# Folding the last chunk's score block and shifting three schedules in a gated attention and MoE kernel

## The chip, the cores and the metric

The kernel runs on one core of a Trainium2 chip. The metric is the device time of one execution in microseconds (us), as the median of several executions. Times of the profile ("span") are some 1.8 us shorter, because they run from the first instruction to the last one. A ratio of two kernels is the mean time of one kernel's runs over that of the other's of the same rounds, so it is not quite the ratio of the medians that are quoted.

## The reference

```python
# u, v: (8, 3008, 256), z: (8, 3008, 64), w_in: (256, 2048), w_out: (2048, 256)
scores = (1.0 / S) * np.matmul(z, z.transpose(0, 2, 1))
attn = np.maximum(scores, 0.0) ** 2
x = (u * np.matmul(attn, v)).reshape(B * S, D)
h = x @ w_in
g = h * (1.0 / (1.0 + np.exp(-1.702 * h)))
return g @ w_out
```

## The kernel before

The scores of a batch are symmetric. Each batch has 3008 rows of z in six chunks of 512 (the last has 448), and a "unit" is two blocks of 128 rows against one chunk: two matmuls of 64 contracted rows (two row tiles that run as a pair), a relu on ScalarE out of PSUM, and a square on VectorE. Blocks below the diagonal are not computed but made by DMA transposes (`tt`), and so is a quarter of each chunk's own block (`ad`, "folded"), except in batch 0 and in the last chunk. The matmuls of the second step, `o`, read a unit as right operand. TensorE runs a fixed list: units are scored ahead, at given "slots" (numbers of `o` steps within a chunk).

```python
    def scores(b, group):
        scs = []
        zt = ZT[b]
        for i, jp in group:
            sc = ps2.tile([P, 2, CH], F32, name="sc", tag="ps2")
            turn = turned(b, i) and jp >= NU - 2
            kp, qi = (2 * i + jp - (NU - 2), NCH - 1) if turn else (jp, i)
            q0, q1 = qi * CH, qi * CH + width(qi)
            if folded(b, i) and jp == 2 * i + 1:
                q0 += CH // 2
            for r in range(2):
                h = slice(r * DQK, (r + 1) * DQK)
                pe.matmul(
                    sc[:, r, :q1 - q0], zt[h, 2 * kp + r, :], zt[h].rearrange("d n p -> d (n p)")[:, q0:q1],
                    start=True, stop=True,
                )
            scs.append(sc)
    # ...
    def square(b, i, jp, sc):
        rl = pw.tile([P, 2, CH], F16, name="rl", tag="rl", bufs=3)
        if folded(b, i) and jp == 2 * i + 1:
            rh = rl[:, :, :CH // 2]
            act.activation(rh, sc[:, :, :CH // 2], AF.Relu, scale=csc)
            dve.tensor_tensor(unit[b, i, jp][:, 1], rh, rh, ALU.mult)
            return
        turn = turned(b, i) and jp >= NU - 2
        n = width(NCH - 1 if turn else i)
    # ...
        a = pa.tile([P, 2, CH], F16, name="a", tag="a", bufs=26)
        unit[b, i, jp] = a
        dve.tensor_tensor(a[:, :, :n], rl[:, :, :n], rl[:, :, :n], ALU.mult)
        if turn:
            twice = rl[:, :, LFULL:LAST]
            dve.tensor_tensor(a[:, :, LAST:], twice, twice, ALU.mult)
    # ...
        half = [(0, TOP, NJ - 1), (1, LOW, NJ - 1)]
        if both:
            order = [[(c, FULL, j)] for j in js[:-CB] for c in cs] + [[(c, FULL, j)] for c in cs for j in js[-CB:]]
            order.insert(-CB, half)
        elif i == full(b):
            order = [[(c, FULL, j)] for c in cs for j in js]
            order.insert(0 if i == NCH - 1 else len(order), half)
    # ...
    def pieces(b, i):

        lst = [(i, jp) for jp in range(2 * i, NU)]
        if i == NCH - 1:
            return [(i, jp) for jp in range(2 * i) if not turned(b, jp // 2)] + lst
        if b == 0:
            return lst[-2:] + lst[:-2] if turned(b, i) else lst
        k = max(len(lst) - 6, 2)
        return lst[:k] + lst[-2:] + lst[k:-2]
    # ...
    SCHED = {
        0: {n: 1 for n in (4, 9, 13, 17, 30, 33, 36, 39, 42, 45)} | {NJ: 2},
        1: {n: 1 for n in (5, 9, 13, 17)} | {NJ: 2},
        2: {n: 1 for n in (2, 7, 12, 17)} | {NJ: 2},
        3: {n: 1 for n in (6, 14, 32, 38)} | {NJ: 2},
        4: {},
        5: NEXT,
    }
    SCHED_LAST = SCHED | {3: {n: 1 for n in (14, 34)} | {NJ: 2}, 4: {NJ: 2}, 5: {}}
    # ...
        2: {n: 1 for n in (0, 3, 7, 11, 28, 32, 36, 40, 44)} | {NJ: 2},
    # ...
    keep_warm(7)
    for g in range(2):
        first_cast(g)
    for copies in [first_zt(g) for g in range(2)]:
        copies()
    posts = scores(0, [queue.pop(0) for _ in range(2)])
    turns = []
    for g in (2, 3):
        first_cast(g)
        keep_warm(2 * g - 2)
        turns.append(first_zt(g))
    for post_ in posts:
        post_()
    turns[0]()
    take(0, 1)
    load_u(0, 1)
```

`SCHED` has an entry for each chunk, in which `n: 1` means: ahead of step n, score one unit, and `NJ: 2` two units ahead of step 24. `SCHED0` (the single line) is for batch 0. Each batch scores two units (10 and 11) of the last chunk's own block. In batches 0 to 6 that is in chunk 3. `SCHED_LAST` is for batch 7, which has no batch after it to score ahead: there both are scored at `4: {NJ: 2}`, step 24 of chunk 4, and chunk 5 begins with `half`, which reads unit 11.

Of the kernel before, what the change touches and what calls it, by code (L numbers as in the profile page):

```python
# [10 lines left out]
F16 = mybir.dt.float16  # L11
P = 128
# [3 lines left out]
def kernel(  # L16
# [13 lines left out]
    AF = mybir.ActivationFunctionType  # L30
    ALU = mybir.AluOpType
# [5 lines left out]
    NJ = (S + P - 1) // P  # L37
    S0 = (S // P) * P
    SREM = S - S0
    CH = 512  # L40
# [12 lines left out]
    csc = 16.0  # L53
# [20 lines left out]
    nil = pw.tile([P, CH], F16, name="nil", tag="gf")  # L74
    dve.memset(nil, 0.0)

    late, LATE = [], []
    ZT, V16, UQ, UT, XT, unit, TT = {}, {}, {}, {}, {}, {}, {}

# [13 lines left out]
    def keep_warm(n):  # L93

        if "w" not in ZT:
            ZT["w"] = ps1.tile([P, CH], F32, name="w", tag="ps1")
        for k in range(n):
            pe.matmul(ZT["w"], nil[:, :P], nil, start=(k == 0), stop=(k == n - 1))  # L98
# [21 lines left out]
    def first_cast(g, by_act=False):  # L120
        m = g % CB * CB
        for c in range(2):
            dst, src = ZT["st"][g // CB][:, m:m + CB, c, :], ZT["f"][g // CB][:, m:m + CB, :]
            if by_act:
                act.activation(dst, src, AF.Copy, scale=1.0)
            else:
                dve.tensor_copy(dst, src)  # L127

    def first_zt(g):

        z2 = ZT["st"][g // CB][:, g % CB * CB:(g % CB + 1) * CB]
        zp = ps1.tile([P, CB, P], F16, name="zp", tag="ps1")
        for k in range(CB):
            pe.transpose(zp[:, k, :], z2[:, k, :, :], ident)  # L134

        def copies():
            zt = ZT[0][:, g * CB:(g + 1) * CB, :].rearrange("d n p -> d (n p)")
            nb = CB if g < NCH - 1 else CB - 1
            dst = zt[:, :nb * P].rearrange("d (p n) -> d p n", n=nb)
            src = zp[:, :nb, :].rearrange("d n p -> d p n")  # L140
            if g in (0, 2, 3):
                act.activation(dst, src, AF.Copy, scale=1.0)  # L142
            else:
                dve.tensor_copy(dst, src)  # L144
            if nb < CB:
                dve.tensor_copy(zt[:, nb * P:], zp[:, nb, :])

        return copies
# [65 lines left out]
    def folded(b, i):  # L214

        return i < NCH - 1 and b > 0

    def turned(b, i):

        return i < NCH - 1 and (b > 0 or i > 3)  # L220
# [6 lines that stand above are left out]
            turn = turned(b, i) and jp >= NU - 2  # L227
            kp, qi = (2 * i + jp - (NU - 2), NCH - 1) if turn else (jp, i)
            q0, q1 = qi * CH, qi * CH + width(qi)
            if folded(b, i) and jp == 2 * i + 1:  # L230
                q0 += CH // 2
            for r in range(2):
                h = slice(r * DQK, (r + 1) * DQK)
# [5 lines that stand above are left out]
        return [lambda u_=u_, sc=sc: square(b, *u_, sc) for u_, sc in zip(group, scs)]  # L239
# [5 lines that stand above are left out]
            act.activation(rh, sc[:, :, :CH // 2], AF.Relu, scale=csc)  # L245
            dve.tensor_tensor(unit[b, i, jp][:, 1], rh, rh, ALU.mult)
            return
        turn = turned(b, i) and jp >= NU - 2
        n = width(NCH - 1 if turn else i)
        act.activation(rl[:, :, :n], sc[:, :, :n], AF.Relu, scale=csc)  # L250
        if folded(b, i) and jp == 2 * i:
            a = pa.tile([P, CB, 2, P], F16, name="a", tag="a", bufs=26)
            unit[b, i, jp] = a
            r4 = rl.rearrange("p r (q c) -> p r q c", q=CB)
            dve.tensor_tensor(a.rearrange("p q r c -> p r q c"), r4, r4, ALU.mult)
            unit[b, i, jp + 1] = pa.tile([P, 2, 2, CH // 2], F16, name="ad", tag="a", bufs=26)
            sp.dma_start_transpose(
                unit[b, i, jp + 1][:, 0].rearrange("p g (r c) -> p (g r) c", c=P),
                a[:, CB // 2:].rearrange("p q r c -> p (q r c)"),
# [5 lines that stand above are left out]
        if turn:  # L265
            twice = rl[:, :, LFULL:LAST]
            dve.tensor_tensor(a[:, :, LAST:], twice, twice, ALU.mult)
        if jp // 2 > i and (turned(b, i) or jp < NU - 2):
            if b and i == 0 and LATE:
                late.append(((jp + 2) % NU, lambda: turn_unit(b, i, jp, a)))  # L270
            elif b == 0 and jp < NU - 2:
                squared.setdefault((i, jp // 2), []).append(lambda: turn_unit(b, i, jp, a))
                while ORDER0 and len(squared.get(ORDER0[0], ())) == 2:
                    for turn_it in squared.pop(ORDER0.pop(0)):
                        turn_it()
            else:
                turn_unit(b, i, jp, a)
# [257 lines left out]
    def store_part(b, k, o, c):  # L535

        r0 = b * S + k * CH
        y = Y[b, k].rearrange("p (m o) c -> p m o c", o=2)[:, :, o, c]
        if o == 0:
            dst = out[r0:r0 + 3 * P].rearrange("(s t) c -> t s c", t=P)[:, ::2, c]  # L540
            sp.dma_start(dst, y)
            return
        sp.dma_start(out[r0 + P:r0 + 2 * P, c], y[:, 0])
        for h in range(2):
            r1 = (b - h) * S + S0
            (act, pool)[h].dma_start(out[r1:r1 + SREM, c], y[h * SREM:(h + 1) * SREM, 1])

    def store(b, k, eng):
        i, n = blocks(b)[k]
# [13 lines left out]
    def pieces(b, i):  # L563
# [8 lines left out]

    NEXT = {n: 1 for n in (2, 6, 11, 15, 33, 37, 41, 45)} | {NJ: 2}
    SCHED = {
        0: {n: 1 for n in (4, 9, 13, 17, 30, 33, 36, 39, 42, 45)} | {NJ: 2},
        1: {n: 1 for n in (5, 9, 13, 17)} | {NJ: 2},
        2: {n: 1 for n in (2, 7, 12, 17)} | {NJ: 2},
        3: {n: 1 for n in (6, 14, 32, 38)} | {NJ: 2},
# [13 lines left out]
    SCHED0 = {  # L592
        0: {2: 1, 6: 2, 14: 2, 22: 2, 30: 2, 38: 2},
        1: {0: 2, 8: 2, 15: 2, 22: 2, 30: 2, 38: 2},
        2: {n: 1 for n in (0, 3, 7, 11, 28, 32, 36, 40, 44)} | {NJ: 2},
        3: {n: 1 for n in (0, 4, 8, 12, 16, 19, 29, 33, 37, 41, 45)} | {NJ: 2},
        4: {},
        5: NEXT,
# [4 lines left out]
    def take(b, n):  # L603
        for post_ in scores(b, [queue.pop(0) for _ in range(n)]):
            post_()
# [17 lines left out]
    for copies in [first_zt(g) for g in range(2)]:  # L623
        copies()
    posts = scores(0, [queue.pop(0) for _ in range(2)])
    turns = []
    for g in (2, 3):
        first_cast(g)
        keep_warm(2 * g - 2)
        turns.append(first_zt(g))  # L630
    for post_ in posts:
        post_()
    turns[0]()
    take(0, 1)
    load_u(0, 1)

    for b in range(B):
# [5 lines left out]
        for i in range(NCH):  # L643
            host = b + 1 if more and i == NCH - 1 else b
            if host > b:
                fill(host)
                LATE.append(host)
            for n, step in enumerate(attend(b, i, b == 0 and i < 2)):
                if b == 0 and i == 0 and n == 5:
                    load_u(0, 0)  # L650
                if b == 0 and i == 0 and n == 3:
                    turns[1]()
                if b == 0 and i == 0 and n in FIRST_CAST:
                    first_cast(FIRST_CAST[n], True)
                if b == 0 and i == 0 and n in FIRST_ZT:
                    first_zt(FIRST_ZT[n])()
                if (i, n) in turn:
                    turn_u(b, turn[i, n])
                if (i, n) in load:
                    load_u(b, load[i, n])  # L660
                if b == 0 and (i, n) in LOADW:
                    load_w(LOADW[i, n])
                if more and (i, n) == (NCH - 2, 2):
                    load_z(b + 1)
                if (b, i, n) == (0, NCH - 1, NJ + 4):
                    for sum_ in weight_sums():
                        sum_()
                take(host, sched[i].get(n, 0))
                if i == full(b) and n >= HEAD and (n - HEAD) * LAGY // (2 * NJ - 10) >= head and head < LAGY:
                    up_group(b, head)  # L670
                    head += 1
                step()
# [58 lines left out]
```

## Time and profile before

| | before |
|---|---|
| median of 3 runs | 1187.44 us (1186.94 to 1187.84) |
| span of the profile | 1186.0 us, mean granted clock 1.000 |
| TensorE busy | 1179.9 us (99%) |
| VectorE, ScalarE busy | 840.9 us (71%), 823.3 us (69%) |

TensorE is never without work for long, so the profile is read as a list of matmul starts: every part of the change must show as a shift of the same matmul between two traces. The lines are in the prediction. In all lines `sc` are the score matmuls, `hg` those with `w_in`, `st` and `yp` those with `w_out`, `rl` is a relu's output, and L234 is line 234 of the kernel.

### The profile page before, as it was taken

How to read it: one execution, taken by the hardware profiler on the slowest of the kernel's cores; microseconds unless marked ns; L12 is line 12 of the kernel's file. 1: busy time of each engine (PE TensorE's matmuls, PEld its weight loads, DVE VectorE, ACT ScalarE, POOL GpSimd, SP SyncE). 2: the span in 40 equal slices, each digit the busy share in tenths (PEclk: the TensorE clock that was granted, in tenths of full speed). 3: DMA queues.
4: the chain of work that ended last, by engine and by line, in shares of the span. 5: the costliest groups of instructions: out<-in, count | busy, mean ns of one | idle time of the engine just before them, and what ended most of it. 6: DMA issues, size and time to landing. Idle time of an engine off the chain costs nothing.

```text
span 1186.0 us, 27884 instructions
## 1 busy us (share of the span) xinstructions
PE 1179.9 (99%) x11529; PEld 723.9 (61%) x11529; DVE 840.9 (71%) x1433; ACT 823.3 (69%) x997; POOL 226.9 (19%) x321
## 2 busy tenths in 40 slices
PE   9999999999999999999999999999999999999998
PEld 3446765467654676547765478554775547855577
DVE  6788865877658776587765878648776587764776
ACT  7878864688646887478764787657876578672785
POOL 5243101231012310133101331014200141001000
PEclk9999999999999999999999999999999999999999
DMA  9997667666778687856789456895659856794012
GB/s 225 188 113 131 129 143 135 79 107 135 143 133 80 108 151 142 132 74 96 159 144 130 75 94 156 153 118 90 111 122 174 100 98 107 137 169 92 1 37 72
DMA packets 374175, 141.82 MB, mean 120 GB/s; under 512 B 315424, under 2 KB 367904, under 8 KB 374048
## 3 DMA queue, kind: packets, MB, share of 16 engines
q1 hardware_dynamic: 315856, 98.34, 45.3%
q0 software_dynamic: 56832, 40.45, 23.1%
q8 instruction: 90, 1.47, 0.5%
q10 hardware_dynamic: 1360, 1.25, 0.3%
q14 instruction: 37, 0.30, 0.1%
HBM read 60.29 MB, written 24.64 MB: 72 GB/s over the span
## 4 chain that ended last, share of the span: by engine, by line
PE 98%; ACT 1%; DVE 1%; issue 0%; DVEq 0%; ACTq 0%
PE o L348 40%; PE hg L389 27%; PE st L508 24%; PE sc L234 6%; PE yp L483 1%; ACT rl L250 1%; PE w L98 0%; PE zp L134 0%; DVE a L264 0%; DVE ut L201 0%; ACT gf L397 0%; DVE zst L127 0%; DVE WT L436 0%; DVE WT L437 0%; DVE ZT L144 0%
## 5 line engine op out<-in xcount | busy, mean ns | idle before, releaser
L397 ACT ACTIVATE gf<-hg 128x1024 f32<-128x1024 f32 (+1 forms) x384 | 385.9, 1005 | 138.6 <-PE hg L389 115.3
L250 ACT ACTIVATE rl<-sc 128x1024 f16<-128x1024 f32 (+1 forms) x309 | 294.9, 991 | 157.2 <-PE sc L234 110.9
L348 PEld LDWEIGHTS <-V 64*128 64x128 f16 (+1 forms) x4052 | 239.0, 94 | 233.7 <-issue 11.8
L389 PE MATMUL hg<-xt,W 128*128 128x512 f16 (+1 forms) x1408 | 354.6, 374 | 0.0
L401 DVE TENSOR_SCALAR gt<-gf 128x1024 f16<-128x1024 f32 (+1 forms) x320 | 223.8, 699 | 133.7 <-ACT gf L397 130.7
L348 PE MATMUL o<-a,V 64*128 64x512 f16 (+3 forms) x2286 | 302.8, 368 | 0.0
L264 DVE TENSOR_TENSOR a<-rl 128x1024 f16<-128x1024 f16 (+1 forms) x274 | 182.9, 671 | 128.7 <-ACT rl L250 128.1
L194 POOL DMA_DIRECT2D uq<-in_u_dram x188 | 127.7, 687 | 692.0 <-PE sc L234 455.7
L348 PE MATMUL o<-tt,V 64*128 64x512 f16 (+1 forms) x1510 | 234.0, 377 | 0.0
L389 PEld LDWEIGHTS <-W 128*128 128x128 f16 x1536 | 139.3, 98 | 119.3 <-issue 2.8
L508 PEld LDWEIGHTS <-gt 128*128 128x128 f16 x2944 | 177.1, 98 | 32.2
L508 PEld LDWEIGHTS <-s 128*128 128x128 f16 x2208 | 133.7, 98 | 25.6 <-issue 0.5
L234 PE MATMUL sc<-ZT 64*128 64x512 f16 (+2 forms) x688 | 118.5, 358 | 0.7 <-ACT ZT L142 0.3
L508 PE MATMUL st<-WT,gt 128*128 128x128 f16 x1472 | 97.8, 219 | 0.0
L508 PE MATMUL st<-WT,s 128*128 128x128 f16 x1472 | 96.5, 219 | 0.2 <-ACT uP L520 0.2
L508 PE MATMUL st<-W,gt 128*128 128x128 f16 x1472 | 96.5, 219 | 0.0
L526 DVE SCALAR_TENSOR_TENSOR y<-st,uP 128x256 f32<-128x256 f32 (+1 forms) x144 | 57.8, 408 | 28.3 <-ACT uP L520 19.9
L520 ACT ACTIVATE uP<-st 128x256 f32<-128x256 f32 (+1 forms) x144 | 53.1, 368 | 31.5 <-DVE y L526 16.2
L365 DVE TENSOR_TENSOR xt<-o,ut 128x512 f16<-128x512 f32 x80 | 51.4, 684 | 23.1 <-PE o L348 23.0
L399 ACT ACTIVATE gt<-gf 128x1024 f16<-128x1024 f32 (+1 forms) x64 | 65.9, 1030 | 2.1
L464 DVE TENSOR_TENSOR s<-s,gt 128x1024 f16<-128x1024 f16 (+1 forms) x96 | 65.0, 677 | 1.1
L462 DVE TENSOR_TENSOR s<-gt 128x1024 f16<-128x1024 f16 (+1 forms) x96 | 64.8, 675 | 0.0
(51 smaller groups left out, 590.9 us busy)
## 6 DMA issues: line engine op xcount, KB each, us to landing
out_dram<-y SPq DMA_DIRECT2D x40, 512.0 KB, 3.6
uq<-in_u_dram POOLq DMA_DIRECT2D x156, 128.0 KB, 3.6
V<-in_v_dram POOLq DMA_DIRECT2D x35, 256.0 KB, 6.4
tt<-a SPq DMA_TRANSPOSE x232, 3.7
uq<-in_u_dram POOLq DMA_DIRECT2D x32, 112.0 KB, 4.8
out_dram<-y SPq DMA_DIRECT2D x7, 384.0 KB, 3.1
vst<-in_v_dram SPq DMA_DIRECT2D x3, 512.0 KB, 5.5
zst<-in_z_dram POOLq DMA_DIRECT2D x7, 192.0 KB, 9.8
```

Source lines behind the costliest of these rows:

```text
L194: eng.dma_start(uq[k * QW:(k + 1) * QW, :n // QW].rearrange("t q c k -> t q (c k)"), src[:, :, cs])
L234: pe.matmul(sc[:, r, :q1 - q0], zt[h, 2 * kp + r, :], zt[h].rearrange("d n p -> d (n p)")[:, q0:q1], start=True, stop=True,)
L250: act.activation(rl[:, :, :n], sc[:, :, :n], AF.Relu, scale=csc)
L264: dve.tensor_tensor(a[:, :, :n], rl[:, :, :n], rl[:, :, :n], ALU.mult)
L348: ins = pe.matmul(acc[c][:, :n], V16[b][h, j].rearrange("p (c k) -> p k c", k=NCC)[:, c], weights(b, i, j)[h], start=(k, m) == first[c], s ...
L389: pe.matmul(hg[:, e, :n], W1[:, c, ff * P:(ff + 1) * P], XT[b, i][:, c, :n], start=(c == 0), stop=(c == NCC - 1),)
L397: act.activation(gf[:, :, :n], hg[:, :, :n], AF.Gelu_apprx_sigmoid, scale=1.0 / FSC)
L399: act.activation(g, gf[:, :, :n], AF.Copy, scale=FSC)
L401: dve.tensor_scalar(g, gf[:, :, :n], FSC, None, ALU.mult)
L462: dve.tensor_tensor(s_, a21, a22, ALU.add)
L464: dve.tensor_tensor(s_, ST[b, k, "S1", h], a11, ALU.subtract)
L508: pe.matmul(bank[:, m, :], lhs()[:, f, m, :], right[:, ff, :], start=name in ("P1", "P2", "P5") and m == 0 and ff == 0, stop=ff == NFF // ...
```

## The change

The intent: fold the last chunk's own block too (unit 11 scores 192 columns instead of 448; the other 256 come from unit 10 through two DMA transposes into a new tile `al`); score one unit of chunk 0 (in batch 0, five units of chunk 2) one step later, where its PSUM buffer is free; put the very first square ahead of later casts, with three warming matmuls fewer (the head); and let ScalarE issue the last remainder stores (the tail).

```diff
--- before.py
+++ after.py
@@ -74,6 +74,7 @@
     nil = pw.tile([P, CH], F16, name="nil", tag="gf")
     dve.memset(nil, 0.0)
 
+    ZP = {}
     late, LATE = [], []
     ZT, V16, UQ, UT, XT, unit, TT = {}, {}, {}, {}, {}, {}, {}
 
@@ -129,7 +130,7 @@
     def first_zt(g):
 
         z2 = ZT["st"][g // CB][:, g % CB * CB:(g % CB + 1) * CB]
-        zp = ps1.tile([P, CB, P], F16, name="zp", tag="ps1")
+        zp = ZP[g] if g in ZP else ps1.tile([P, CB, P], F16, name="zp", tag="ps1")
         for k in range(CB):
             pe.transpose(zp[:, k, :], z2[:, k, :, :], ident)
 
@@ -227,7 +228,7 @@
             turn = turned(b, i) and jp >= NU - 2
             kp, qi = (2 * i + jp - (NU - 2), NCH - 1) if turn else (jp, i)
             q0, q1 = qi * CH, qi * CH + width(qi)
-            if folded(b, i) and jp == 2 * i + 1:
+            if jp == 2 * i + 1 and (folded(b, i) or i == NCH - 1):
                 q0 += CH // 2
             for r in range(2):
                 h = slice(r * DQK, (r + 1) * DQK)
@@ -245,7 +246,12 @@
             act.activation(rh, sc[:, :, :CH // 2], AF.Relu, scale=csc)
             dve.tensor_tensor(unit[b, i, jp][:, 1], rh, rh, ALU.mult)
             return
-        turn = turned(b, i) and jp >= NU - 2
+        if i == NCH - 1 and jp == NU - 1:
+            n = LAST - CH // 2
+            act.activation(rl[:, :, :n], sc[:, :, :n], AF.Relu, scale=csc)
+            dve.tensor_tensor(unit[b, i, jp][:, :, CH // 2:LAST], rl[:, :, :n], rl[:, :, :n], ALU.mult)
+            return
+        turn = jp >= NU - 2 and (turned(b, i) or i == NCH - 1)
         n = width(NCH - 1 if turn else i)
         act.activation(rl[:, :, :n], sc[:, :, :n], AF.Relu, scale=csc)
         if folded(b, i) and jp == 2 * i:
@@ -265,6 +271,10 @@
         if turn:
             twice = rl[:, :, LFULL:LAST]
             dve.tensor_tensor(a[:, :, LAST:], twice, twice, ALU.mult)
+        if i == NCH - 1 and jp == NU - 2:
+            ad = unit[b, i, jp + 1] = pa.tile([P, 2, CH], F16, name="al", tag="a", bufs=26)
+            for r in range(2):
+                sp.dma_start_transpose(ad[:, :, r * P:(r + 1) * P], a[:, r, CH // 2:])
         if jp // 2 > i and (turned(b, i) or jp < NU - 2):
             if b and i == 0 and LATE:
                 late.append(((jp + 2) % NU, lambda: turn_unit(b, i, jp, a)))
@@ -543,7 +553,7 @@
         sp.dma_start(out[r0 + P:r0 + 2 * P, c], y[:, 0])
         for h in range(2):
             r1 = (b - h) * S + S0
-            (act, pool)[h].dma_start(out[r1:r1 + SREM, c], y[h * SREM:(h + 1) * SREM, 1])
+            act.dma_start(out[r1:r1 + SREM, c], y[h * SREM:(h + 1) * SREM, 1])
 
     def store(b, k, eng):
         i, n = blocks(b)[k]
@@ -572,7 +582,7 @@
 
     NEXT = {n: 1 for n in (2, 6, 11, 15, 33, 37, 41, 45)} | {NJ: 2}
     SCHED = {
-        0: {n: 1 for n in (4, 9, 13, 17, 30, 33, 36, 39, 42, 45)} | {NJ: 2},
+        0: {n: 1 for n in (5, 9, 13, 17, 30, 33, 36, 39, 42, 45)} | {NJ: 2},
         1: {n: 1 for n in (5, 9, 13, 17)} | {NJ: 2},
         2: {n: 1 for n in (2, 7, 12, 17)} | {NJ: 2},
         3: {n: 1 for n in (6, 14, 32, 38)} | {NJ: 2},
@@ -592,7 +602,7 @@
     SCHED0 = {
         0: {2: 1, 6: 2, 14: 2, 22: 2, 30: 2, 38: 2},
         1: {0: 2, 8: 2, 15: 2, 22: 2, 30: 2, 38: 2},
-        2: {n: 1 for n in (0, 3, 7, 11, 28, 32, 36, 40, 44)} | {NJ: 2},
+        2: {n: 1 for n in (0, 3, 7, 11, 29, 33, 37, 41, 45)} | {NJ: 2},
         3: {n: 1 for n in (0, 4, 8, 12, 16, 19, 29, 33, 37, 41, 45)} | {NJ: 2},
         4: {},
         5: NEXT,
@@ -623,15 +633,16 @@
     for copies in [first_zt(g) for g in range(2)]:
         copies()
     posts = scores(0, [queue.pop(0) for _ in range(2)])
-    turns = []
-    for g in (2, 3):
-        first_cast(g)
-        keep_warm(2 * g - 2)
-        turns.append(first_zt(g))
-    for post_ in posts:
-        post_()
-    turns[0]()
+    first_cast(2)
+    keep_warm(2)
+    copies = first_zt(2)
+    posts[0]()
+    first_cast(3)
+    posts[1]()
     take(0, 1)
+    keep_warm(1)
+    copies()
+    ZP[3] = ps1.tile([P, CB, P], F16, name="zp", tag="ps1")
     load_u(0, 1)
 
     for b in range(B):
@@ -648,8 +659,10 @@
             for n, step in enumerate(attend(b, i, b == 0 and i < 2)):
                 if b == 0 and i == 0 and n == 5:
                     load_u(0, 0)
+                if b == 0 and i == 0 and n == 2:
+                    copies = first_zt(3)
                 if b == 0 and i == 0 and n == 3:
-                    turns[1]()
+                    copies()
                 if b == 0 and i == 0 and n in FIRST_CAST:
                     first_cast(FIRST_CAST[n], True)
                 if b == 0 and i == 0 and n in FIRST_ZT:
```

## The prediction

> **What bounds the kernel now.** I read the page first, then the waits of TensorE, then the timeline around the places that the diff touches, and at last the start times of single matmuls.
>
> From the page, engine shares and the chain that ended last:
>
> ```profile
> PE 1179.9 (99%) x11529; PEld 723.9 (61%) x11529; DVE 840.9 (71%) x1433; ACT 823.3 (69%) x997; POOL 226.9 (19%) x321
> ...
> PE 98%; ACT 1%; DVE 1%; issue 0%; DVEq 0%; ACTq 0%
> ```
>
> TensorE is the bound from 1.2 us to 1182 us. Work taken from VectorE or ScalarE pays nothing by itself; only fewer matmul columns, or a wait of TensorE removed, moves the end. The table of TensorE's waits seems to say that no waits are left:
>
> ```profile
> PE w L98 <- DVE nil L75: 1.2, 1, 1.2
> PE sc L234 <- ACT ZT L142: 0.3, 1, 0.3
> PE zp L134 <- DVE zst L127: 0.2, 1, 0.2
> PE st L508 <- ACT uP L520: 0.2, 1, 0.2
> PE sc L234 <- ACT rl L250: 0.2, 1, 0.2
> ```
>
> (us in total, times, longest.) It understates them. A matmul's modelled duration (0.376 us for 512 columns) is longer than the spacing at which the next follows (0.216 us), so a wait of up to 0.16 us disappears wholly under the tail of the matmul before, and a longer one mostly. The timeline of TensorE and of ScalarE at the start of the second batch's chunk 0:
>
> ```profile
> 161.10 0.60 PE L234 MATMUL sc<-ZT 64*128 64x512 f16 x4
> 161.54 1.03 PE L348 MATMUL o<-a,V 64*128 64x512 f16 x8
> 162.61 0.39 PE L234 MATMUL sc<-ZT 64*128 64x512 f16 x2
> ...
> 161.53 2.86 ACT L250 ACTIVATE rl<-sc 128x1024 f16<-128x1024 f32 x3 [0.50 <-PE sc L234]
> ```
>
> Two score units (four matmuls, two row tiles each) go out at 161.10; four pairs of `o` follow at 0.216 us a pair, so the third unit could start at 161.54 + 4 x 0.216 = 162.41. It starts at 162.61. Score tiles have two PSUM buffers, and the first is free only when ScalarE's first relu ends, about 161.53 + 1.02 = 162.55. So 0.20 us are lost. Going through all matmul starts for spacings over the usual one, I find this same 0.41 us step from `o` to `sc` eight times: seven at 162.2, 309.6, 454.1, 601.5, 746.0, 893.5 and 1038.0 us (chunk 0 of batches 1 to 7) and once at 44.9 us (middle of chunk 2 of batch 0, also four slots behind a double unit).
>
> **What the Trainium skill says.** "TensorE: Matmul & The Clock Gate", section "Back-to-back issue gap", gives N/2.4 + 2.5 ns between warm matmuls, 216 ns at 512 columns. The trace agrees (0.216 us at 512, 0.056 us at 128), not with the lower sustained figure of 131 ns at 512 in the same section. Its section "The mechanism" has matmuls in different row groups overlap, started some 4 ns apart: here 3 to 4 ns, or about 20 ns in stretches after a wait, with an unchanged 0.216 us a pair. "Perfetto Trace Analysis", section "Identifying the Most-Contended Engine", warns that matmul busy time is no good measure for TensorE; the eight hidden waits above are an example. "DMA: Bandwidth & Descriptors", section "Rules for kernel authors", advises to issue a DMA early and wait late, so that its fixed cost overlaps; the new transposes do that in batches 0 to 6, and hardly in batch 7.
>
> **The change, part by part.**
>
> *1. One slot later.* The third unit of chunk 0 moves behind a fifth pair of `o`: 161.54 + 5 x 0.216 = 162.62, just past the release seen at 162.61. The wait is gone by a hair, the work is the same. The list for chunk 2 of batch 0 moves 28 to 29 in the same way. 8 x 0.20 = 1.6 us. The next units then have 0.2 us less behind them; by the relu times (about 0.92 us apart) the fourth wants to start at 163.70 and its buffer is free at about 163.5, so no new wait.
>
> *2. The fold.* The last chunk scores its own units 10 and 11 with 448 columns each. Unit 11 keeps columns 256 to 447, 192 of them; the other 256 come from unit 10 by two DMA transposes. TensorE's saving is read where all neighbours are row-tiled:
>
> ```profile
> 88.80 0.27 PE L234 MATMUL sc<-ZT 64*128 64x256 f16 x2
> 88.91 1.11 PE L348 MATMUL o<-a,V 64*128 64x448 f16 x10
> ...
> 94.88 0.35 PE L234 MATMUL sc<-ZT 64*128 64x448 f16 x2
> 95.06 0.92 PE L348 MATMUL o<-a,V 64*128 64x448 f16 x8
> ```
>
> A pair of 256 columns costs 0.11 us, one of 448 columns 0.19 (row starts 94.875 to 95.065), both columns/2.4 + 3 ns; 192 columns are then 0.083. Saved 0.106 us a batch, 8 x 0.106 = 0.85 us. Both weight loads of a pair run side by side (94 ns, started 3 ns apart), so I don't expect them to limit. ScalarE saves some 0.45 us and VectorE about nothing (0.3 us off the square, 0.22 us for the new copy of 64 columns) per batch: off the path. SP gets 16 more transposes, none of which delays another use that is near, except this one:
>
> *3. The price, in the last batch.* Batches 0 to 6 score units 10 and 11 in chunk 3 and use them in chunk 5, over 10 us later. Batch 7 scores both in the middle of chunk 4, and chunk 5 begins with the half block, which reads unit 11:
>
> ```profile
> 1088.67 0.56 PE L234 MATMUL sc<-ZT 64*128 64x448 f16 x4
> 1089.05 3.63 PE L348 MATMUL o<-tt,V 64*128 64x512 f16 x32
> 1089.07 1.73 ACT L250 ACTIVATE rl<-sc 128x896 f16<-128x896 f32 x2 [7.26 <-PE sc L234]
> ...
> 1090.02 0.63 DVE L264 TENSOR_TENSOR a<-rl 128x896 f16<-128x896 f16 x1 [5.03 <-ACT rl L250]
> ...
> 1094.01 0.66 PE L348 MATMUL o<-a,V 64*128 64x448 f16 x3
> ```
>
> Square from 1090.02, copy (0.22 us) to 1090.8, first transpose issued at 1090.84. An issue holds SP 1.2 us (`ad`, four blocks of 128x128: 1.19 to 1.22), so the second starts at 1092.0. Four blocks land 2.4 to 2.5 us after their issue begins, eight blocks 3.2 to 3.4, so two blocks land after about 2.0 (an estimate from that slope): 1094.05, and with the input loads that land until 1094.3 rather 1094.2. The half block wants to run at 1094.01 - 0.11 = 1093.90. A new wait of 0.3 us (0 to 0.8), once.
>
> *4. The head.* Three of six warming matmuls (0.216 us each) go; the first square is put in front of the casts of z group 3. Before: casts end 7.57, first square 7.50 to 8.17, first `o` at 8.55. After: square as soon as the first relu ends (6.93), done at about 7.65; third score unit at 7.14 instead of 8.23, first `o` at 7.69. But from there ScalarE is the limit:
>
> ```profile
> 8.66 0.02 ACT rl L250
> 8.69 0.85 issue
> 9.54 0.02 ACTq L250
> 9.55 0.03 issue
> 9.58 1.02 ACT rl L250
> ```
>
> (the chain that ended last, in order of time). ScalarE was idle 0.33 us before 8.66, waiting for that third unit, and is then without a pause to 15.97. Taking relus back to back from 7.73, its fourth relu ends at 10.16 instead of 10.60 and the sixth at 13.08 instead of 13.53, and the eighth score unit, which waits for it, comes at 13.11 instead of 13.58. So of the 0.9 us that the first `o` gains, 0.45 us last.
>
> *5. The tail.* Both remainder stores go to ScalarE (0.54 us issue each), which puts its copy for P4 from 1181.29 to about 1181.45. The last store, on SP, is issued at 1182.63 and lands at 1184.49; ScalarE's second store would be issued near 1182.35 and land near 1184.6. I count 0 (-0.2 to +0.2).
>
> Sum: 1.6 + 0.85 + 0.45 - 0.3 + 0 = 2.6 us. 1187.44 - 2.6 = 1184.8 us.
>
> **The rivals.** (a) The moved slot doesn't help: ScalarE's release moves along, or the wait turns up at the following unit. For it: the margin is 0.015 us, the buffers are two. Against it: the relu chain starts from the first unit, which the move leaves alone, and the later releases have 0.2 us. It would leave the time at 1186.4. (b) The transposes cost more than estimated: SP's queue is in order, they compete with the loads of u, and `ad` landings up to 4.4 us exist. A landing of 4 us for the second would make the wait 2.2 us, and the time 1186.7. (c) The head gives its gain back: transposes and V casts have their own clocks, and chunk 1 might wait for them; or it keeps all 0.9 us. Time 1185.3 or 1184.4. (d) Two per cent either way would be 24 us; no part touches more than 2 us, and a wait in every batch over 3 us on the new tiles would be needed, where 10 us lie between.
>
> **Range and chances.** The main sum is good to about 0.5 us at part 3, 0.3 at parts 1, 2, 4 and 5 each; the three runs of before spread over 0.9 us. That gives 1183.8 to 1186.0. Faster or slower by over 2%: below half a per cent each.
>
> **What would show it.** Right: the step from the fourth `o` pair of chunk 0 to `sc` gone in all batches; 16 `sc` matmuls of 192 columns, 0.083 us a pair; first `o` near 7.7 us and the eighth score unit near 13.1; in batch 7 a gap of some 0.3 us before chunk 5's half block, released by a transpose. Wrong: a gap at a later unit of chunk 0, a pair of 192 columns that takes 0.11 us, a gap of over 1 us in batch 7, a last store of ScalarE that lands past 1184 minus the shift by more than 0.2 us, or any wait for the transposes in batches 0 to 6.

## The result, and the profile after

The changed kernel took 1187.17 us (median of 6, 1186.86 to 1189.36) and the kernel before, in the same rounds, 1187.69 us (1186.94 to 1187.97). The ratio is 1.0000, with an interval of 0.9987 to 1.0013: the same time, where 2.6 us less were predicted. The execution that was profiled was one of the slower ones (1188.29 us; span 1186.5 us).

The page of the changed kernel, engine shares and chain that ended last:

```profile
PE 1176.8 (99%) x11526; PEld 699.6 (59%) x11526; DVE 837.7 (71%) x1441; ACT 819.3 (69%) x997; POOL 226.6 (19%) x319
...
PE 96%; ACT 1%; DMA 1%; issue 1%; DVE 1%; SPq 0%; DVEq 0%; ACTq 0%
```

TensorE is busy 3.1 us less, and the span is 0.5 us more: matmul work went, and waiting came. The chain now has DMA in it, which it had not before. TensorE's waits say where (us in total, times, longest):

```profile
PE o L358 <- DMA tt<-a: 1.8, 1, 1.8
PE o L358 <- DMA al<-a: 1.8, 1, 1.8
```

Two waits of 1.8 us each, both for a DMA transpose, are new. The first is in no term of the predicted sum (the prediction has a wait for transposes in batches 0 to 6 only among the signs that it is wrong); the second was predicted at 0.3 us. The shift of the same matmul between the two traces gives the account (changed minus before, us):

| stretch | shift gained or lost in it | shift at its end |
|---|---|---|
| start to the 97th `o` matmul (38 us) | -0.77 | -0.77 |
| batch 0, slot in chunk 2 | -0.20 | -0.97 |
| batch 0, wait for `tt` (+2.0) and 192 columns (-0.11) | +1.89 | +0.92 |
| batch 0, a step near 85 us that is gone | -0.11 | +0.81 |
| batches 1 to 6, slot and 192 columns | -1.93 (0.32 each) | -1.12 |
| batch 7, slot and 192 columns | -0.30 | -1.42 |
| batch 7, wait for `al` | +2.01 | +0.59 |
| tail | -0.10 | +0.49 |

**The slot.** TensorE and ScalarE at the start of batch 1's chunk 0, changed kernel (start, duration, engine, group):

```profile
161.91 0.61 PE L235 MATMUL sc<-ZT 64*128 64x512 f16 x4
...
162.35 2.85 ACT L256 ACTIVATE rl<-sc 128x1024 f16<-128x1024 f32 x3 [0.50 <-PE sc L235]
162.36 1.24 PE L358 MATMUL o<-a,V 64*128 64x512 f16 x10
...
163.44 0.38 PE L235 MATMUL sc<-ZT 64*128 64x512 f16 x2
```

Five pairs of `o` start at 162.36, and 162.36 + 5 x 0.216 = 163.44 is just where the third unit starts. The 0.20 us step is gone; all eight such steps are.

**The fold.** Where the 448 columns of unit 11 were, in batch 0, and the group of these matmuls over the whole kernel (count, then busy us and mean ns):

```profile
63.56 0.26 PE L235 MATMUL sc<-ZT 64*128 64x192 f16 x2
...
63.64 0.93 PE L358 MATMUL o<-a,V 64*128 64x512 f16 x5
```

```profile
L235 PE MATMUL sc<-ZT 64*128 64x192 f16 x16 | 2.0, 243 | 0.0
```

There are 16 of 192 columns, and the next pair starts 0.08 us after one (63.56 to 63.64), as predicted. The 243 ns are the modelled duration, which includes the pipeline, and not the cost.

**The head.** The chain that ended last, start of the changed kernel (start, duration, what):

```profile
10.80 1.96 ACT rl L256 x2
12.76 0.04 issue
12.81 0.39 PE sc L235 x2
```

The eighth score unit starts at 12.81 us; before it was 13.58. The first relu, which the change does not touch, started earlier in this execution as well, at 5.58 instead of 5.91. So 0.445 us of the 0.77 lie between the first relu and the eighth unit (7.226 us instead of 7.671), and 0.33 us ahead of the first relu.

**The last batch.** The changed kernel around the end of chunk 4 of batch 7:

```profile
1088.31 2.50 POOL L195 DMA_DIRECT2D uq<-in_u_dram  x4 [8.05 <-PE sc L235]
1088.69 0.63 DVE L270 TENSOR_TENSOR a<-rl 128x896 f16<-128x896 f16 x1 [5.03 <-ACT rl L256]
1089.24 0.22 DVE L273 TENSOR_TENSOR a<-rl 128x128 f16<-128x128 f16 x1
...
1089.51 2.47 SPq L277 DMA_TRANSPOSE al<-a  x2
...
1091.95 0.81 PE L358 MATMUL o<-tt,V 64*128 64x512 f16 x6
...
1094.60 0.37 PE L358 MATMUL o<-al,V 64*128 64x448 f16 x2 [1.83 <-DMA al<-a]
```

Square, copy and the issue of the two transposes come as fast as predicted: the second issue begins near 1090.74, and the half block could start at 1092.60 (six matmuls, three pairs, from 1091.95), 1.86 us later; 1.90 had been worked out. But it starts at 1094.60. The transposes landed 4.0 and 3.7 us after their issue; the estimate for the second had been 2.2. At the same time GpSimd issues the four transfers of the last load of u.

The same stretch of batch 0, where there was no wait before:

```profile
53.78 0.35 PE L235 MATMUL sc<-ZT 64*128 64x448 f16 x2
...
55.98 0.82 PE L358 MATMUL o<-tt,V 64*128 64x512 f16 x6 [1.84 <-DMA tt<-a]
```

The transpose that it waits for was issued at 47.92 us and landed at 55.94, 8.0 us later; the same one in the kernel before was issued at 42.26 and landed at 46.73, 4.5 us later.

### The profile page after: what moved, and what is told of

It reads as the page before. It is cut to its first block, busy times and chain, and to the rows that moved or that the text cites. A ratio compares the mean times of both kernels' runs of the same rounds, so it can differ in the third digit from the quotient of the medians.

```text
span 1186.5 us, 27918 instructions
## 1 busy us (share of the span) xinstructions
PE 1176.8 (99%) x11526; PEld 699.6 (59%) x11526; DVE 837.7 (71%) x1441; ACT 819.3 (69%) x997; POOL 226.6 (19%) x319
## 4 chain that ended last, share of the span: by engine, by line
PE 96%; ACT 1%; DMA 1%; issue 1%; DVE 1%; SPq 0%; DVEq 0%; ACTq 0%
PE o L358 39%; PE hg L399 27%; PE st L518 24%; PE sc L235 5%; ACT rl L256 1%; DMA tt<-a 1%; PE yp L493 1%; DMA al<-a 0%; PE w L99 0%; DVE a L270 0%; ACT ZT L143 0%; SPq L277 0%; DVE ut L202 0%; ACT gf L407 0%; DVE WT L446 0%
## 5 line engine op out<-in xcount | busy, mean ns | idle before, releaser
L256 ACT ACTIVATE rl<-sc 128x1024 f16<-128x1024 f32 (+1 forms) x301 | 287.7, 993 | 153.7 <-PE sc L235 108.4
L358 PEld LDWEIGHTS <-V 64*128 64x128 f16 (+1 forms) x4052 | 218.0, 95 | 257.9 <-issue 16.3
L358 PE MATMUL o<-a,V 64*128 64x512 f16 (+3 forms) x2240 | 296.1, 368 | 0.2 <-DVE a L270 0.2
L270 DVE TENSOR_TENSOR a<-rl 128x1024 f16<-128x1024 f16 (+1 forms) x266 | 178.5, 675 | 123.3 <-ACT rl L256 122.6
L235 PE MATMUL sc<-ZT 64*128 64x512 f16 (+3 forms) x688 | 114.6, 356 | 0.7 <-ACT ZT L143 0.4
```

The source lines that it names most:

```text
L235: pe.matmul(sc[:, r, :q1 - q0], zt[h, 2 * kp + r, :], zt[h].rearrange("d n p -> d (n p)")[:, q0:q1], start=True, stop=True,)
L256: act.activation(rl[:, :, :n], sc[:, :, :n], AF.Relu, scale=csc)
L358: ins = pe.matmul(acc[c][:, :n], V16[b][h, j].rearrange("p (c k) -> p k c", k=NCC)[:, c], weights(b, i, j)[h], start=(k, m) == first[c], s ...
```

## The experiments

Nine kernels ran, in three groups, each group on one chip with the kernel before. Kernel before + head + slots + fold + tail gives the changed kernel exactly, so parts can be undone and done alone. The letters in the quoted texts are theories. A: the parts are worth what was predicted, and the loss is in the two waits; that of batch 7 comes from scoring late in it, that of batch 0 from the new head. C, later C2: the wait in batch 0 is an accident of an execution, which any version can have or not. A2, for the last run: the landing in batch 7 is long because the load of u is on the way at the same time; B2: it is as long whatever else runs. What other letters stand for is told where they are.

| kernel | median us (range, runs) | before, same group | ratio to before (95%) |
|---|---|---|---|
| e1_early_last | 1185.45 (1185.11 to 1186.91, 5) | 1187.62 | 0.9984 (0.9972 to 0.9995) |
| e2_old_head | 1188.90 (1187.38 to 1189.10, 5) | 1187.62 | 1.0008 (0.9995 to 1.0021) |
| e3_slot_only | 1186.45 (1186.02 to 1188.21, 5) | 1187.62 | 0.9993 (0.9981 to 1.0005) |
| e4_fold_only | 1189.09 (1188.51 to 1193.55, 6) | 1187.62 | 1.0017 (1.0006 to 1.0028) |
| e5_head_only | 1188.04 (1187.25 to 1194.28, 6) | 1187.91 | 1.0007 (0.9987 to 1.0027) |
| e6_slots_fold_early | 1185.79 (1185.64 to 1186.12, 5) | 1187.91 | 0.9978 (0.9964 to 0.9993) |
| e7_quiet_last | 1187.25 (1186.60 to 1191.53, 6) | 1187.91 | 1.0000 (0.9981 to 1.0018) |
| e8_after_again | 1187.33 (1186.79 to 1187.37, 5) | 1187.91 | 0.9990 (0.9975 to 1.0004) |
| e9_load_behind | 1187.24 (1186.11 to 1192.95, 6) | 1187.88 | 0.9995 (0.998 to 1.001) |

Differences are below 0.3%, so the times alone decide little; each verdict rests on shifts of matmuls in one trace per kernel. The result of every kernel was right.

### e1_early_last: the changed kernel, with batch 7's last units scored early

```diff
-    SCHED_LAST = SCHED | {..., 4: {NJ: 2}, 5: {}}
+    SCHED_LAST = SCHED | {..., 4: {8: 1, 14: 1}, 5: {}}
```

> The changed kernel, but the last batch scores units 10 and 11 of its last chunk at slots 8 and 14 of chunk 4 instead of both at slot 24. Theory A (half of the missing gain is the wait of chunk 5's half block for the second transpose in batch 7, 1.9 us in the trace, and it is only a matter of when it is issued): no wait for al, every other step as in the changed kernel, time 1.9 us below the changed kernel's 1187.2, so about 1185.3. Rival B (the wait only moves: the scores now wait for ScalarE or for a buffer of ring a, or the transposes delay the transposes of chunk 4): less than 0.7 us gained, and a new wait in batch 7.

Batch 7 of this kernel:

```profile
1083.92 0.25 PE L235 MATMUL sc<-ZT 64*128 64x192 f16 x2
...
1084.61 2.46 SPq L277 DMA_TRANSPOSE al<-a  x2
...
1091.42 0.35 PE L358 MATMUL o<-al,V 64*128 64x448 f16 x2
```

The second transpose has over five microseconds, and the half block starts with no wait. There is no wait in batch 0 either, although the head is the new one. The shift to the kernel before is -2.57 us at batch 6, -2.61 at the last matmul of batch 7, -2.41 at the end, and the medians differ by 2.17 us. By the trace this is nearly the 2.6 us that the prediction had promised for the changed kernel; by the medians 0.4 us less. A small price is visible: at step 24 of chunk 4, 0.28 us are lost where TensorE waits for a signal of GpSimd that the two score units had hidden.

### e2_old_head: the changed kernel, with the head of before

```diff
-    first_cast(2); keep_warm(2); copies = first_zt(2); posts[0]() ...
+    for g in (2, 3): first_cast(g); keep_warm(2 * g - 2); turns.append(first_zt(g)) ...
```

> The changed kernel with the head of before (order of first casts and squares, six warming matmuls). Theory A (the 1.9 us wait for a transpose tt in chunk 3 of batch 0 comes from the head being earlier, which lets u loads and transposes collide more): no wait for tt in batch 0, time 1187.2 + 0.8 (head gain lost) - 1 to 1.9 (wait gone), so 1186.1 to 1187, with a smaller spread than the 2.5 us of the changed kernel. Rival C (the wait is an accident of the DMA queues that any version has in some executions, before included): wait for tt seen again or the spread stays over 2 us; mean 0.8 us above the changed kernel.

The wait in batch 0 is not there, which A expects, but e1, with the new head, has none either; that alone takes the head part of A away. The time is 1188.90 us, more than A allowed, because the wait for `al` has its full size and has a sequel. Stretches of batch 7 in e2 (start:end, length, busy us and counts of TensorE, its weight loads, VectorE, ScalarE and GpSimd, granted clock, DMA share, GB/s):

```profile
1088.90:1092.90 4.00, 2.33 (x22) 0.88 (x18) 1.73 (x3) 0.00 (x0) 0.37 (x1) 1.00 0.48 118
1092.90:1094.50 1.60, 1.37 (x7) 0.63 (x8) 0.00 (x0) 0.00 (x0) 0.00 (x0) 0.99 0.00 0
1094.50:1097.90 3.40, 3.40 (x10) 1.36 (x9) 0.69 (x1) 1.34 (x2) 0.00 (x0) 0.50 0.00 0
1097.90:1101.00 3.10, 3.10 (x17) 1.47 (x15) 1.58 (x3) 2.25 (x3) 0.00 (x0) 1.00 0.00 0
```

The wait of 1.9 us runs from 1091.23 to 1093.13, 0.23 us into the second stretch. 1.3 us after its end the granted clock falls to 0.50 for 3.4 us, which costs 1.7 us: the shift goes from -0.88 at the first `hg` of batch 7 to +0.81. The same wait in the changed kernel, e4, e7 and e8 had no such sequel in the traced execution. Four of the five runs of e2 lie at 1188.80 to 1189.10 us with a mean clock of 0.998, the fifth at 1187.38 with 0.999, so most of them may have had it.

The clock records of the kept traces show what sets e2 apart. In all eleven traces the granted clock, once it has first risen, changes only a whole number of steps of 3.413 us later (in e2 it rises at 5.61 us and changes 319 and 320 steps on, at 1094.47 and 1097.88). Of the nine waits of TensorE over 1 us after the start, the one of e2 lay whole within one such step, 1.91 us, and one of e9 had 2.29 us in one; half clock followed both at the end of that step. Of the other seven no step held more than 1.80 us (e7), and none was followed by half clock. So what counted here is the part of a wait within one step. That the border lies between 1.80 and 1.91 us is an inference from nine waits.

### e3_slot_only: the kernel before, with the two slot lists

```diff
-        0: {n: 1 for n in (4, 9, 13, 17, 30, ...
+        0: {n: 1 for n in (5, 9, 13, 17, 30, ...
-        2: {n: 1 for n in (0, 3, 7, 11, 28, 32, 36, 40, 44)} | {NJ: 2},
+        2: {n: 1 for n in (0, 3, 7, 11, 29, 33, 37, 41, 45)} | {NJ: 2},
```

> The kernel before with the moved slots alone. Theory A: all eight 0.2 us steps from o to sc gone, nothing new, 1.6 us faster than before (1186.1 against 1187.7). Rival: the wait turns up again later or chunk 2 of batch 0 (slots 29 to 45) makes the transposes of batch 0 late: 0 to 1 us.

-0.20 us in batch 0, and from +1.92 to +0.43 in batches 1 to 7, which is -0.21 in each: the slots are worth 1.7 us in this trace. A further 0.11 us go near 85 us, where all traces with slots or fold are so much ahead of before, and e5 is not. It was not foreseen; the kept traces show a wait for ScalarE that goes. Before, an `hg` matmul starts 0.33 us after the matmul ahead of it, at 84.54, just when the gelu that it waits for has ended (84.48); in e4 that gelu ends at 84.17, and the matmul starts without a pause at 84.32. The medians differ by 1.17 us only. Between batch 0's slot and 85 us the shift rises from -0.18 to +2.02. This is a wait which the traced execution had and the others may or may not have had:

```profile
PE hg L389 <- DMA W<-in_moe_w_in_dram: 2.1, 1, 2.1
```

So also a kernel with the old head and no fold can wait 2 us for a DMA in batch 0, here for weights.

### e4_fold_only: the kernel before, with the fold

```diff
-            if folded(b, i) and jp == 2 * i + 1:
+            if jp == 2 * i + 1 and (folded(b, i) or i == NCH - 1):
...
+            for r in range(2):
+                sp.dma_start_transpose(ad[:, :, r * P:(r + 1) * P], a[:, r, CH // 2:])
```

> The kernel before with the fold alone. Theory A: 0.11 us saved a batch, 0.9 us, and the wait of about 2 us for al in batch 7 against it: about 1.0 us slower than before (1188.7). Rival (the al wait came from the other parts having moved batch 7 against the u loads): wait 0.3 us or less, 0.5 us faster.

-0.105 us a batch, as predicted, and -0.84 at the start of batch 7 with the 0.11 near 85 us. Then the last 0.105 and the wait, which is 2.1 us by this shift: +1.18 after it and +1.3 at the end:

```profile
PE o L357 <- DMA al<-a: 1.9, 1, 1.9
```

The fold alone is 1.5 us slower than the kernel before (medians), and the interval excludes 1. With its transposes issued where they are, it costs over twice what it saves.

### e5_head_only: the kernel before, with the new head

The edit is the diff of the head above, with `ZP`, and nothing else.

> The kernel before with the head alone. Prediction's step: 0.45 us gained at the 96th o matmul. The traces so far: -0.77 and -0.22 us with the new head, -0.31, 0.02 and 0.00 with the old one, against the kernel before. Theory H1 (the head is worth about 0.3 us on average, and the moment at which the clock goes to full speed, 4.0 to 6.6 us, moves each execution by as much): 0.1 to 0.6 us faster than before. Rival H2 (worth 0.8): 1187.0 or less by the same runs of before. Rival C of the first call (the head makes batch 0 wait for DMAs more often): waits of TensorE for DMA in batch 0 in this trace, time equal to before or slower.

1188.04 us against 1187.91: no gain in time. From the first relu to the eighth score unit it is 7.227 us instead of 7.671, the predicted 0.445 us; but the first relu starts at 6.13 instead of 5.91, so that the eighth unit and the 97th `o` are 0.23 us early only. The shift stays at -0.15 from 94 us to the last `st`, and the tail, which is that of before, ends 0.06 us late.

### e6_slots_fold_early: slots, fold and early scoring, head and tail of before

The edit is that of e3, e4 and e1 on the kernel before.

> The kernel before with slots, fold, and the early scores of the last batch; old head and old tail stores. By the traces, 1.65 + 0.84 = 2.5 us faster than before without a wait for al: 1185.1 against 1187.6. If head and tail are worth about 0.2 us together, e1_early_last's 1185.45 would be equal to it within the noise.

1185.79 us, -2.12 in medians, though the traced execution waited 0.5 us for a `tt` in batch 0. The shift is -1.97 at batch 6 and -2.03 at the end, so batch 7 no longer loses. Head and tail, left out here, are not missed.

### e7_quiet_last: the changed kernel, with the last load of u later in the program

```diff
+        if not more:
+            load = {(3, NJ + 20): 4, (4, NJ + 22): 5}
+            turn = {k: v for k, v in TURN.items() if v < 5} | {(5, 12): 5}
```

> The changed kernel, but in the last batch the u load of chunk 5 is issued at slot 46 of chunk 4 (not 29), and turned at slot 12 of chunk 5, so that no u load is under way while the two al transposes are. Theory A2 (al lands 3.7 to 4.0 us after its issue because the u load fills the DMA engines; alone, as the first one in the run with the early scores, it lands after 2.3): second al after 2.0 to 2.4, the wait in batch 7 shrinks from 1.9 to 0.2 to 0.5 us, time about 1.5 us under the changed kernel. Rival B2 (two transposes one behind the other take 3.8 us whatever else runs): wait stays over 1.3 us.

The edit did nothing to what it aimed at, and the run tells nothing of the load's part. The load went out before the transposes, as in the changed kernel:

```profile
1086.88 2.50 POOL L195 DMA_DIRECT2D uq<-in_u_dram  x4 [8.05 <-PE sc L235]
...
1088.09 2.46 SPq L277 DMA_TRANSPOSE al<-a  x2
```

GpSimd's own list has nothing between the old place of the load and the new one. In both kernels it stands behind the same signal (L86), which followed TensorE's step 23 of chunk 4 at 1086.13 us here, and the load began 0.75 us later. The buffer was no hindrance: its last reader on VectorE had ended at 1068.73. The wait for `al` was the same 1.8 us, and the time 1187.25 us.

### e8_after_again: the changed kernel with only a comment added

> The changed kernel again, unchanged. Theory A: the wait for al of 1.8 to 2.0 us is there again. Theory C2 (the wait for tt in batch 0 is an accident of one execution, since e1_early_last has the same batch 0 and did not wait): no wait for tt of the same size at the same place; and where the 1.9 us wait for al is followed by a stretch of half clock, as in e2_old_head, some 1.7 us more.

No wait for `tt` in batch 0, and again the wait for `al`:

```profile
PE o L358 <- DMA al<-a: 1.8, 1, 1.8
```

The shift is -0.23 at the 97th `o`, -0.55 at the first `hg` of batch 0, -2.32 at batch 6, -0.63 in batch 7 and -0.43 at the end. This is the account of a usual execution of the changed kernel, and it agrees with the medians (1187.33 against 1187.91, -0.58).

### e9_load_behind: the changed kernel, with batch 7's last load of u on SP's queue

```diff
-        eng = pool if b or i else sp
+        eng = sp if (b, i) in ((0, 0), (B - 1, NCH - 1)) else pool
```

SP issues in order, so the load now follows the two transposes.

> The changed kernel, but the last batch's u load of chunk 5 is issued from SP, whose queue keeps its order: it comes behind both al transposes. (e7_quiet_last moved only its place in the program; POOL ran ahead and issued it at the same moment, so that it tested nothing.) Theory A2 (the u load of 448 rows fills the DMA engines just when the al transposes are issued): first al lands after 2.3, second after 2.3 to 2.5 us unless an instruction fetch hits, as in the runs with early scores; the wait in batch 7 shrinks from 1.8 to 0.4 to 0.7 us, time 1.2 us under the changed kernel, 1186.0. Rival B2 (the second of two transposes takes 3.7 us whatever else runs, as 3.9 in batch 0): wait stays over 1.3 us. A wait of VectorE for the later u load must not show.

Batch 7 of e9:

```profile
1094.53 2.46 SPq L277 DMA_TRANSPOSE al<-a  x2
...
1097.16 2.01 SPq L195 DMA_DIRECT2D uq<-in_u_dram  x4
...
1099.01 0.37 PE L358 MATMUL o<-al,V 64*128 64x448 f16 x2 [1.23 <-DMA al<-a]
```

DMA in the 6 us around the transposes of the changed kernel, and then the 5 us around those of e9 (for queues: packets, MB, share of the 16 engines; for issues: count, median us to landing):

```profile
q14 instruction: 1, 0.01, 0.3%
...
al<-a SPq DMA_TRANSPOSE x2, 3.9
```

```profile
q14 instruction: 1, 0.01, 0.6%
...
al<-a SPq DMA_TRANSPOSE x2, 2.7
```

With the load out of the way, the median landing falls from 3.9 to 2.7 us (the second transpose from 3.7 to 3.1) and the wait from 1.8 to 1.2 (by the shift, 2.0 to 1.4). B2 falls: the landing is not fixed. A2 is right in kind and too large in size; the load is not all.

What is the rest? A transpose counts as landed when its semaphore has all 16 increments. The Trainium skill, "DMA: Bandwidth & Descriptors", section "Why a DMA increments its semaphore by 16 and not by 1", has up to 16 engines finish independently, and only the full 16 mean that all has landed. The trace agrees, and shows what it costs. In e9, 15 of the 16 increments of the second transpose came by 2.37 us after its issue, and the last at 3.13; an 8 KB packet of the instruction queue began 1.58 us after the issue and took 0.46 us. In the five traces with the load beside (the changed kernel, e2, e4, e7, e8) 15 came by 3.02 to 3.16 us and the last at 3.70 to 3.81, each with one such packet. In e1 and e6 a 16 KB and an 8 KB packet met the second transpose: two increments were late, the last at 4.5 and 4.1 us, and nobody waited for it.

So the estimate of about 2.0 to 2.2 us was near for 15 increments with nothing else running, the load of u adds 0.65 us to them in the changed kernel, and one instruction packet 0.7 us (0.57 to 0.76 in six traces) to the sixteenth. The part of the load is shown by e9. The part of the packet is read from the traces and no run took the packet away; nor do the records name a packet's DMA engine. But the counts bear it out: nine `al` transposes with neither load nor packet had all 16 increments by 2.29 to 2.35 us. Of the four-block `ad` transposes, six had a packet that began 1.8 us or more after the issue, and each had one late increment; 23 whose packet began within 1.1 us had none. One of the six is in the trace of before: the `ad` landing of 4.4 us, which the prediction mentions, had 15 increments by 2.44 us.

The same skill, "Runtime: NRT & Kernel Launch", section "Instruction fetch mechanics", calls the cost of such fetches "mostly hidden" (it speaks of 16 KiB blocks). Hidden from the engine that fetches they may be; here the packet lies on the path of another engine's transpose.

e9 is not the better kernel for it (1187.24 us): its traced execution, at 1192.95 us, had a wait of 3.9 us for `tt` in batch 0, with 6.8 us of half clock after it.

## Why the prediction was wrong, point by point

1. **Slots, -1.6 predicted: right.** All eight steps went, with 0.20 to 0.22 us each, -1.7 in all; e3 shows it alone.
2. **Fold, -0.85 predicted: right.** 0.08 us for a pair of 192 columns, and eight times 0.105 us in the changed kernel, -0.84; e4, the fold alone, has -0.81.
3. **The price in batch 7, 0.3 (0 to 0.8) predicted: this is the step that failed.** It is the term "two blocks land after about 2.0 ... rather 1094.2", 2.2 us after the issue. The mechanism was named and everything up to the issue was right to 0.04 us; the landing took 3.7 to 3.8 us, and the wait was 2.0 to 2.1 us by the shift in the changed kernel and in e2, e4, e7 and e8. Of the excess of 1.7 us, 0.5 are the load of u beside it (0.65 where 0.15 had been allowed), 0.7 the instruction packet, 0.3 the landing of 15 increments without any company (2.37 where the slope gave 2.05), and 0.14 us pass from landing to the matmul. The slope from eight to four to two blocks was taken from landings in quiet places. It was somewhat short even there, gave the load of u a quarter of its weight, and left the instruction packet out. Rival (b) of the prediction, a landing of 4 us and 1186.7 us, was nearly this case (1187.17), and it was given too little room in the range.
4. **Head, -0.45 predicted: right in the stretch that was computed, and half of it not there on average.** From the first relu to the eighth unit it is 7.225 to 7.230 us in all six traces with the new head, against 7.671 in the profile of before, from which the 0.45 was computed. The old head varies here, from 7.31 (e2) to 7.67 in five traces, so that one trace was too few. But in five of the six traces with the new head, the first relu itself starts later than before (5.96 to 6.13 instead of 5.91), though the instructions ahead of it are the same. It goes with the moment at which the clock first becomes full (5.62 to 6.62 us there, 5.24 before, 3.98 in the profiled run of the changed kernel, whose first relu is at 5.58), and so it does with the old head (e3: 5.88, first relu 6.09). At the 97th `o` the six traces with the new head are 0.22 to 0.77 us early (0.34 on average), the five with the old one between 0.31 early and 0.02 late (0.11 early on average). About 0.2 us are left, and e5's time shows none of it. Whether the later clock is chance or comes of the head stays open: six traces do not tell.
5. **Tail, 0 predicted: right.** From the last `st` matmul to the end, new tail minus before is between -0.10 and +0.20 us in six traces, and kernels with the old tail scatter from -0.04 to +0.21. Inside it one estimate was off: seen from the last `st`, ScalarE's copy for P4 moved back by 0.37 us, not by 0.16.

The sum for a usual execution is then -1.67 for slots, -0.84 for the fold, -0.11 near 85 us, -0.23 for the head and +2.0 for the wait: -0.85, which is the shift of e7 at its last `st` (-0.83). With 0.2 us of scatter in the tail, e7 ends at -0.66 and e8 at -0.43; the medians of the changed kernel say -0.52 (first rounds) and -0.58 (e8). It is the wait of batch 7 that took the gain: with the transposes early, e1 has the same sum without the 2.0 and with 0.28 for GpSimd's signal, -2.57, and its last `st` is at -2.61.

**In no term of the sum: waits in batch 0.** Five traced executions have the very same program in batch 0 (the changed kernel, e1, e7, e8, e9). Their wait for `tt` there was 1.8, 0, 0, 0 and 3.9 us. Of the five traces with the old head, before, e2 and e4 had none, e6 had 0.5 us, and e3 the 2.1 us for weights. So theory A fell in its part on the head: these waits come and go between executions. That loads of u and of weights are under way beside the transposes there is seen in the traces; what decides which execution loses is not settled. The +0.5 us of the profiled execution is this accident, and not what the change costs.

**The upper runs.** The kernel before too had runs of 1191.71 and 1193.22 us, at a mean clock of 0.998, and so had e4, e5, e7 and e9. e2 and e9 show one way into it: a wait of 1.9 or 3.9 us, and then half clock. That the untraced runs went the same way is an inference.

Of the signs that the prediction had named as showing it wrong, two were there: the gap of over 1 us in batch 7, in all five traces with the late transposes and the load beside, and in three traces a wait for a transpose in batch 0.

## What to carry to other kernels

Before moving work from TensorE to a DMA, find the use that comes soonest after the issue, and give it the worst landing of that kind of transfer seen in a busy stretch, not the median of the quiet ones; one late use of eight took 2.0 of some 2.8 us. The cure cost one line: scoring the two units some steps earlier in the last batch gives 1185.45 us with the whole change (e1), and 1185.79 us with slots and fold alone (e6), both ahead of both kernels, and the ratios do not separate the two. Where the whole effect is some 0.2%, compare the start of the same instruction in two traces and take more than one trace: one execution in some has a wait of its own.

## What the Trainium skill lacked or had wrong

- "DMA: Bandwidth & Descriptors" tells why only the full 16 increments count, but not what that does to short transfers in company: 15 of 16 by 2.37 us and the last at 3.13 in e9, 3.02 to 3.16 and 3.70 to 3.81 in the five traces with the load of u beside.
- No page gives the time to landing of small DMA transposes: an issue holds SP for some 1.2 us whether it moves two, four or eight blocks of 128x128 (at the least 1.17, 1.19 and 1.23 us); two blocks land after 2.3 us alone, four after 2.4 to 2.5, eight after 3.1 to 3.4 at their shortest, and two beside the load of u in batch 7 after 3.7 to 4.1.
- "Runtime: NRT & Kernel Launch", "Instruction fetch mechanics": fetches are called mostly hidden. Packets of 8 KB (0.3 to 0.7 us) and of 16 KB (0.9 to 1.4 us) go with one late increment each of a transpose that another engine waits for, late by some 0.7 us here and by 2.1 us in e1.
- "TensorE: Matmul & The Clock Gate", "HAM oscillation — how this bites in real kernels", sums the rule up as no idle gaps of TensorE over some 3.4 us. In e2 a wait of 1.9 us was enough for 3.4 us at half clock, which began 1.3 us after the wait had ended; it lay whole within one 3.41 us step of the clock's changes. In four other traces, where at most 1.8 us of the same wait fell into one step, it was not.
